# Up products with differences of weights, and a list scheduler that orders all engines

## The chip, the cores and the metric

The kernel runs on one core of one Trainium2 chip. The metric is the device time of one execution in microseconds (us). Three timed runs of the kernel before took 1724.11, 1726.66 and 1726.99 us; the median is 1726.66 us.

The engines are TensorE (PE; its weight loads are shown as PEld), VectorE (DVE), ScalarE (ACT), GpSimd (POOL) and SyncE (SP), whose queue issues transfers and, in this kernel, carries the marks between the two halves of a product. SBUF is the working memory and PSUM, with 8 banks of 128 x 512 float32, is where matmuls write.

## The reference

A causal convolution with weights of its own for each token and head is followed by a maxout layer.

```python
w = softmax(weight_gen, axis=-1)                      # 8 x 4160 tokens, 8 heads, 7 taps
out[b, s, h, :] = sum_k w[b, s, h, k] * x_pad[b, s + k, h, :]   # 192 = 8 heads x 24
x = out.reshape(33280, 192)
h = np.maximum(np.maximum(x @ w1, x @ w2), x @ w3)    # each weight 192 x 768
return h @ w_out                                      # 768 x 192
```

All is float32, and so is the result.

## The kernel before

**Tiles.** The 33280 tokens lie as 128 rows with 260 tokens each. Four tokens of each row, 512 in all, are a chunk, and there are 65 chunks; up to three chunks share the loading of x and of the tap weights and one softmax (a super). For each of the chunk's four token columns GpSimd multiplies taps and x (`product`, L244) and VectorE sums over the taps (`total`, L259). The sums are turned so that the 192 features lie on the partitions: the first three chunks on TensorE (L274, L275), the others by VectorE's transpose of 32 x 32 blocks (L282) and 24 small moves on ScalarE (L288).

**Parts.** TensorE multiplies in a short format (`F32R`), so each factor is split in a high part and a low part, and a product is high x high, low x high and high x low. `parts` makes them of x (L298 to L307): `xa_hi` and `xa_lo` for the first 128 features, and for the remaining 64, which fill only half of the partitions, `xb` and `xc` that hold the high part twice and the low part beside it. The weights are split once, at the start, by `split` (L459 to L487): ScalarE, six VectorE operations, ScalarE and GpSimd on each piece. They come as 8 byte words (`words`), so the splitting works on bits.

**Products.** Every product runs as two halves of 64 rows of the array: first the lower half's matmuls into a bank of PSUM, then the upper half's into the same bank. While the upper half of one product runs, the lower half of the next does. Between the two halves of one product stands an empty instruction on SyncE (L336), which waits for the lower half's last matmul and which the upper half's first waits for. `up` makes 18 products of 512 columns for a chunk, one for each of three weights and six blocks of 128 of the 768 columns, with 4 or 5 matmuls per half. `down` makes four, one for each token column, with twelve per half: `h_hi` against both parts of w_out side by side (384 columns) and `h_lo` against the high part (192).

**Maxout.** `maximum` empties the bank of the first weight by a ScalarE copy into `m` (L374), and takes the maxima with the second and the third on VectorE (L376). Then ScalarE casts `m` to `h_hi` (L379) and GpSimd subtracts to get `h_lo` (L383). A down sum's two column groups are added by ScalarE (L406) and VectorE (L407) and leave with one transfer for a chunk (L411).

**What sets the order.** Each engine runs its instructions in the order in which the program writes them (`pin`). That order is laid out by ticks: a chunk has 22, one for each half of a double product and one for each down sum, and constants name the chunk and the tick at which each stage is written (`PRODUCTS`, `SUMS`, `TRANSPOSE`, `PARTS`, `SOFTMAX`, `LOAD`). The first four chunks and the splitting of the weights have a table of their own, `OPENING`. The down sums of a chunk stand in the middle of the next one's up products (`DOWN_AT`). `lower` and `advance_upper` interleave the two halves by `SLOTS`. 

## Time and profile before

| | before |
|---|---|
| timed runs | 1724.11, 1726.66, 1726.99 us |
| span of the profiled execution, first to last instruction | 1723.8 us |
| PE busy | 1675.3 us, 97%, 16794 matmuls |
| PE weight loads busy | 1653.3 us, 96% |
| DVE busy | 1135.9 us, 66% |
| ACT busy | 1138.4 us, 66% |
| POOL busy | 1428.0 us, 83% |
| mean granted TensorE clock | 0.992 |
| moved by DMA | 79.50 MB, 46 GB/s in the mean |

The page gives the span of the profiled execution, and the three runs' device times beside it lie 0.3 to 3.2 us above. Matmuls overlap, so a busy PE says that matmuls were under way, not at what pace; the pace is read from the starts in the timeline. Groups of instructions are shown with count, total busy time and mean ns of one, and behind the bar with the idle time in front of them and what ended it. Stretches show the busy time of PE, PEld, DVE, ACT and POOL in a piece of the span, then the granted clock, the share of the DMA engines and GB/s.

### The profile page before, as it was taken

Reading aid. Unit: us, or ns where it says so; the run is one execution under the profiler, and the core shown is the slowest. Engines: PE = TensorE matmul, PEld = TensorE weight load, DVE = VectorE, ACT = ScalarE, POOL = GpSimd, SP = SyncE. Lnnn points to the kernel's source line nnn. Section 1 sums busy time; section 2 is a strip of 40 time slices with the busy share of each in tenths; the row PEclk is TensorE's granted clock in tenths of the full one; section 3 lists DMA queues with packets and bytes.
Section 4 is the critical chain, followed back from the end, with each engine's and each line's share of the span. In section 5 each row is a group of like instructions: output and inputs, shape, how many; then the busy total and the mean of one; then the engine's idle time right before and its main releaser. Section 6 shows DMA issues by size and latency. Waiting matters only on the chain.

```text
span 1723.8 us, 42110 instructions
## 1 busy us (share of the span) xinstructions
PE 1675.3 (97%) x16794; PEld 1653.3 (96%) x16794; DVE 1135.9 (66%) x1570; ACT 1138.4 (66%) x2878; POOL 1428.0 (83%) x844
## 2 busy tenths in 40 slices
PE   3789999999999999999999999999999999999998
PEld 2589999999999999999999999999999999999998
DVE  7976666666666666766666666666666666666652
ACT  4456676667667667666766766766676676676662
POOL 5788888988888888888888898988889888888852
PEclk9899999999999999999999999999999999999999
DMA  7010101101010101101010110101011010101000
GB/s 232 1 60 20 69 11 69 62 27 60 20 69 10 69 35 45 69 20 69 11 69 20 60 69 19 60 20 69 19 61 69 20 60 20 69 11 46 19 18 21
DMA packets 19989, 79.50 MB, mean 46 GB/s; under 512 B 2272, under 2 KB 4568, under 8 KB 17104
## 3 DMA queue, kind: packets, MB, share of 16 engines
q1 hardware_dynamic: 19672, 76.54, 11.6%
q8 instruction: 131, 2.15, 0.5%
q14 instruction: 66, 0.54, 0.1%
q10 hardware_dynamic: 120, 0.28, 0.1%
HBM read 51.25 MB, written 25.56 MB: 45 GB/s over the span
## 4 chain that ended last, share of the span: by engine, by line
PE 95%; DVE 3%; DMA 1%; ACT 1%; issue 0%; SPq 0%; POOL 0%; POOLq 0%; DVEq 0%; ACTq 0%
PE ph L327 95%; DVE acc L259 1%; DVE m L376 0%; DMA h_lo<-in_moe_w_dram 0%; DVE e L484 0%; DVE ph L480 0%; DVE ph L463 0%; DVE ph L475 0%; DVE ph L468 0%; DMA xt<-in_x_dram 0%; DVE ph L461 0%; SPq L518 0%; ACT ph L459 0%; ACT f L486 0%; PE ph L274 0%
## 5 line engine op out<-in xcount | busy, mean ns | idle before, releaser
L244 POOL TENSOR_TENSOR r<-xt,wt 128x1344 f32<-128x1344 f32 x260 | 721.9, 2816 | 1.9 <-DVE acc L259 1.4
L376 DVE TENSOR_TENSOR m<-ph,m 128x512 f32<-128x512 f32 x780 | 522.8, 684 | 219.7 <-PE ph L327 121.7
L383 POOL TENSOR_TENSOR h_lo<-m,h_hi 128x512 fp32r<-128x512 f32 x390 | 503.1, 1301 | 166.8 <-ACT h_hi L379 162.0
L327 PE MATMUL ph<-xa_hi,wa_hi 64*128 64x512 f32 x2340 | 628.6, 391 | 10.9 <-ACT f L486 7.0
L327 PE MATMUL ph<-xa_hi,wa_lo 64*128 64x512 f32 x2340 | 625.3, 389 | 5.8 <-POOL wa_lo L487 5.8
L327 PE MATMUL ph<-xa_lo,wa_hi 64*128 64x512 f32 x2340 | 625.0, 388 | 0.0
L327 PE MATMUL ph<-xb,wb_hi 64*128 64x512 f32 x2340 | 624.3, 388 | 0.0
L327 PE MATMUL ph<-wo,h_hi 64*128 64x384 f32 x3120 | 597.9, 360 | 0.2 <-DVE m L376 0.2
L327 PE MATMUL ph<-wo,h_lo 64*128 64x192 f32 x3120 | 556.6, 250 | 1.6 <-POOL h_lo L383 1.6
L379 ACT CAST h_hi<-m 128x512 fp32r<-128x512 f32 x390 | 241.9, 621 | 406.5 <-DVE m L376 403.4
L327 PEld LDWEIGHTS ph<-wo,h_hi 64*128 64x128 f32 x3120 | 488.6, 185 | 6.5 <-issue 1.0
L327 PEld LDWEIGHTS ph<-wo,h_lo 64*128 64x128 f32 x3120 | 487.1, 189 | 2.1 <-POOL h_lo L383 2.1
L259 DVE TENSOR_REDUCE acc<-r 128x192 f32<-128x1344 f32 x260 | 401.7, 1546 | 111.7 <-POOL r L244 111.7
L327 PE MATMUL ph<-xc,wb_lo 64*128 64x512 f32 x1170 | 453.6, 388 | 0.0
L288 ACT COPY room<-room 32x128 f32<-32x128 f32 x1488 | 440.6, 296 | 19.3 <-DVE room L282 1.2
L327 PEld LDWEIGHTS ph<-xa_hi,wa_hi 64*128 64x128 f32 x2340 | 366.3, 185 | 15.3 <-ACT f L486 8.2
L327 PEld LDWEIGHTS ph<-xa_hi,wa_lo 64*128 64x128 f32 x2340 | 358.6, 185 | 9.3 <-POOL wa_lo L487 7.9
L327 PEld LDWEIGHTS ph<-xa_lo,wa_hi 64*128 64x128 f32 x2340 | 359.0, 185 | 1.8 <-DVE xa_lo L302 0.4
L327 PEld LDWEIGHTS ph<-xb,wb_hi 64*128 64x128 f32 x2340 | 358.7, 185 | 1.4
L374 ACT COPY m<-ph 128x512 f32<-128x512 f32 x390 | 221.5, 585 | 60.5 <-PE ph L327 51.8
L407 DVE TENSOR_TENSOR o<-ph,ob 128x192 f32<-128x192 f32 x260 | 86.5, 352 | 238.5 <-ACT ob L406 238.5
L327 PEld LDWEIGHTS ph<-xc,wb_lo 64*128 64x128 f32 x1170 | 216.6, 185 | 1.2 <-issue 0.2
(57 smaller groups left out, 700.8 us busy)
## 6 DMA issues: line engine op xcount, KB each, us to landing
xt<-in_x_dram SPq DMA_DIRECT2D x20, 1728.0 KB, 6.9
out_dram<-o SPq DMA_DIRECT2D x65, 384.0 KB, 2.3
wt<-in_weight_gen_dram SPq DMA_DIRECT2D x21, 336.0 KB, 3.0
h_hi<-in_moe_w_dram SPq DMA_DIRECT2D x6, 256.0 KB, 5.2
xt<-in_x_dram SPq DMA_DIRECT2D x1, 1536.0 KB, 9.5
h_lo<-in_moe_w_dram SPq DMA_DIRECT2D x6, 192.0 KB, 5.2
room<-in_moe_w_out_dram SPq DMA_DIRECT2D x1, 1152.0 KB, 8.4
xt<-in_x_dram SPq DMA_DIRECT2D x1, 960.0 KB, 5.7
```

The lines of the kernel that those rows point to most:

```text
L244: nc.gpsimd.tensor_tensor(r.rearrange("p (h g) k -> p k h g", g=G), xt[:, la + t : la + t + K].rearrange("p k (h g) -> p k h g", g=G), wt[ ...
L259: nc.vector.tensor_reduce(state["acc", c][:, t], r, axis=AX.X, op=ALU.add)
L288: pin(nc.scalar.copy(to[:, :, p : p + 32], blocks[p : p + 32, :, f : f + 32]))
L327: ins = nc.tensor.matmul(ph[:, :n], w[h], v[h], start=half == 0 and q == 0, stop=half == 1 and q == len(terms) - 1,)
L374: pin(nc.scalar.copy(m[:, :N], ph[:, :N]))
L376: pin(nc.vector.tensor_tensor(m[:, :N], ph[:, :N], m[:, :N], op=ALU.max))
L379: later(1, lambda: pin(nc.scalar.copy(hi, m[:, :N])))
L383: nc.gpsimd.tensor_tensor(lo, m[:, :N], hi.bitcast(F32), op=ALU.subtract)
L407: pin(nc.vector.tensor_tensor(o[:, t], po[:, :D], ob, op=ALU.add))
```

## The change

**Arithmetic.** max(x w1, x w2, x w3) is x w1 + max(0, x (w2 - w1), x (w3 - w1)). So only two up products are made for each block, with the differences of the weights, and the first is emptied by a rectified copy on ScalarE (L859). The part x w1 reaches the output as x (w1 w_out): the 192 x 192 matrix w1 w_out is made once (`turn_weights`, `compose`) and three matmuls per half with the parts of x join each down sum (`wca`, `wcb`). The weights are needed as float32 for that: `single` rebuilds a float32 value from the words (ScalarE and four VectorE operations), GpSimd subtracts, ScalarE and GpSimd split.

**Emptying PSUM.** The second product's maximum (L867) is written back to its bank for four of the six blocks, and ScalarE's cast (L871) and the subtraction for `h_lo` (L878), which is then VectorE's, read it there. For blocks 1 and 4 (`ON_POOL`) it goes to `m`, and GpSimd subtracts as before.

**Loading.** Two chunks share x, tap weights and softmax instead of three. The second pieces of the weights are loaded in two groups (6 + 6 transfers instead of 6), w_out in three. Two chunks instead of three are turned on TensorE. The half of the partitions on which `xb` and the low part lie changes from chunk to chunk (`low`), which saves a copy of ScalarE (L306 of before).

**Order.** `OPENING` and the tick constants are gone. Each operation is a `Task` with an engine, a cost, the tasks that it needs, the buffers that it holds and a due time; `Plan.order` plays the engines through and starts, on each free engine, the ready task of earliest due time whose buffers are free. The two halves of TensorE are two engines there (L and U) and keep the order in which they are written. The instructions are then written in the order of these starts.

```diff
-OPENING = {
-    -1: (
...
-TICKS = 22
-PRODUCTS = ((2, 5), (2, 7), (2, 13), (2, 16))
-SUMS = ((2, 8), (2, 12), (2, 18), (1, 2))
-TRANSPOSE = ((1, 4), (1, 5), (1, 6), (1, 7), (1, 10), (1, 11), (1, 12))
-PARTS = ((1, 13), (1, 14), (1, 15))
-SOFTMAX = ((4, 13), (4, 20), (3, 13), (3, 15))
...
+        def can(t):
...
+                    h.taken = True
+                    self.free[h.pool] -= 1
+            t.start = now
+            done.append(t)
+            busy[t.engine] = now + t.cost
+            heapq.heappush(events, (now + t.cost, 0, t.n, t, "free"))
+            heapq.heappush(events, (now + t.end, 1, t.n, t, "given"))
+            heapq.heappush(events, (now + t.end + self.LATENCY, 2, t.n, t, "seen"))
+        now = 0.0
+        while True:
+            for e in ready:
+                if busy[e] > now + 1e-9:
+                    continue
+                if e in self.FIXED:
+                    k = at[e]
+                    if k < len(self.waiting[e]):
+                        t = self.waiting[e][k]
+                        if t.missing == 0 and can(t):
+                            at[e] += 1
+                            start(t, now)
+                    continue
+                heap, kept = ready[e], []
+                while heap:
+                    x = heapq.heappop(heap)
+                    if can(x[2]):
+                        start(x[2], now)
+                        break
+                    kept.append(x)
+                for x in kept:
+                    heapq.heappush(heap, x)
+            if not events:
+                break
+            now = events[0][0]
+            while events and events[0][0] <= now + 1e-9:
+                _, _, _, t, what = heapq.heappop(events)
+                if what == "given":
+                    for h in t.holds:
+                        h.users -= 1
+                        if h.users == 0:
+                            self.free[h.pool] += 1
+                elif what == "seen":
+                    for a in t.after:
+                        a.missing -= 1
+                        if a.missing == 0 and a.engine not in self.FIXED:
+                            heapq.heappush(ready[a.engine], (a.due, a.n, a))
+        assert len(done) == len(self.tasks), (len(done), len(self.tasks))
...
+    NI = 2
+    SC = 2
+    TS = SC * TC
+    ON_TENSOR = 2
+    DOWN_AT = 3
+    ON_POOL = (1, 4)
...
+            p = plan.add(
+                "POOL", 2.75, product, [ready[s], *loads[s][1]], due - 26 + 3 * t, [hr, hx, hw]
+            )
+            sums.append(plan.add("DVE", 1.55, total, [p], due - 22 + 3 * t, [hr, ha]))
...
+        lo = plan.add(name, cost, a_low, [hi], due - 1.5, [al, ah, *hs])
+        bl = plan.add(name, cost, b_low, cs, due - 1.4, [b, k, *hs])
...
+        a = plan.add(
+            "ACT", act(n),
+            lambda: pin(nc.scalar.activation(u(), high().bitcast(F32), AF.Abs)),
+            deps, due, [hb, hc, *holds],
+        )
...
+        return plan.add(
+            "DVE", vec(n),
+            lambda: pin(
+                nc.vector.scalar_tensor_tensor(
+                    target().bitcast(U32), low(), 29, ui(),
+                    op0=ALU.logical_shift_right, op1=ALU.bitwise_or,
+                )
+            ),
+            [d], due, [hb, hc, *holds],
+        )
...
+            d = plan.add(
+                "POOL", gps(2 * P),
+                lambda mine=mine: pin(
+                    nc.gpsimd.tensor_tensor(mine(), mine(), w1a[:, pair], op=ALU.subtract)
+                ),
+                [got, one_a[jp]], due - 3, [hx],
+            )
...
+            b = buf(hb)
+            pin(nc.tensor.transpose(b[:, :P], w1a[:, j], ident))
+            for to in (P, P + DB):
+                pin(nc.tensor.transpose(b[:, to : to + DB], b32[h, jp, 0], ident[h, h]))
+        got = plan.add("L", 0.5, turn, [one_a[jp], one_b[jp], made, *u_last()], 0, [hb], end=0.8)
...
+            def mult(hb=hb, at=at):
+                for j in range(NJ):
+                    pin(
+                        nc.tensor.matmul(
+                            buf(hb)[:, :D], w1t()[:, j, at : at + P], wo32[:, j],
+                            start=j == 0, stop=j == NJ - 1,
+                        )
+                    )
+            got = plan.add("L", 2.4, mult, deps + u_last(), 0, [hb, hw1t], end=2.8)
...
-            state["m", j] = mp.tile([P, CH], F32, name="m", bufs=4)
-        m = state["m", j]
-        if i == 0:
-            pin(nc.scalar.copy(m[:, :N], ph[:, :N]))
-        else:
-            pin(nc.vector.tensor_tensor(m[:, :N], ph[:, :N], m[:, :N], op=ALU.max))
-        if i == 2:
-            hi, lo = h_hi[:, j, :N], h_lo[:, j, :N]
-            later(1, lambda: pin(nc.scalar.copy(hi, m[:, :N])))
-            later(
-                2,
-                lambda: pin(
-                    nc.gpsimd.tensor_tensor(lo, m[:, :N], hi.bitcast(F32), op=ALU.subtract)
-                ),
-            )
+        def terms(half):
+            got = [
+                (CH, lambda: wa_hi[:, j, i], lambda: buf(ah), [w_hi[jp, i], hi], [ah]),
+                (CH, lambda: wa_hi[:, j, i], lambda: buf(al), [w_hi[jp, i], lo], [al]),
+                (
+                    (CH, lambda: wb_hi[:, j, i], lambda: buf(b), [*b_hi[j], bl], [b])
+                    if half == low
+                    else (CH, lambda: wb_hi[:, j, i], lambda: buf(k), [*b_hi[j], *cs], [k])
+                ),
+                (CH, lambda: wa_lo[:, j, i], lambda: buf(ah), [w_lo[jp, i], hi], [ah]),
+            ]
+            if half == odd:
+                got.append((CH, lambda: wb_lo[:, jp, i], lambda: buf(k), [b_lo[jp], *cs], [k]))
...
+        if i == 0:
+            hs[c, j, 0] = plan.add(
+                "ACT", act(CH),
+                lambda: pin(nc.scalar.activation(buf(hm), buf(hb), AF.Relu)), [made], due,
+                [hb, hm],
+            )
+            return
+        on_pool = j in ON_POOL
+        keep = hm if on_pool else hb
+        m = plan.add(
+            "DVE", vec(CH),
+            lambda: pin(nc.vector.tensor_tensor(buf(keep), buf(hb), buf(hm), op=ALU.max)),
+            [made, hs[c, j, 0]], due, [hb, hm],
+        )
+        his[j] = plan.add(
+            "ACT", act(CH), lambda: pin(nc.scalar.copy(buf(hh)[:, j], buf(keep))), [m], due + 1,
+            [keep, hh],
+        )
+        eng = nc.gpsimd if on_pool else nc.vector
+        los[j] = plan.add(
+            "POOL" if on_pool else "DVE", gps(CH) if on_pool else vec(CH),
+            lambda: pin(
+                eng.tensor_tensor(
+                    buf(hl)[:, j], buf(keep), buf(hh)[:, j].bitcast(F32), op=ALU.subtract
+                )
+            ),
+            [his[j]], due + 2, [keep, hh, hl],
+        )
...
-            terms += [(2 * D, h_hi[:, j, sl], wo[:, j]), (D, h_lo[:, j, sl], wo[:, j, :D])]
+        def terms(half):
+            got = [
+                (2 * D, lambda: buf(ah)[:, sl], lambda: wca, first, [ah]),
+                (D, lambda: buf(al)[:, sl], lambda: wca[:, :D], first, [al]),
+                (
+                    (D, lambda: buf(b)[:, sl], lambda: wcb[:, :D], first, [b])
+                    if half == low
+                    else (2 * D, lambda: buf(k)[:, sl], lambda: wcb, first, [k])
+                ),
+            ]
+            for j in range(NJ):
+                got.append(
+                    (
+                        2 * D, lambda j=j: buf(hh)[:, j, sl], lambda j=j: wo[:, j],
+                        [his[j], o_hi[j], o_lo[j]], [hh],
+                    )
+                )
+                got.append(
+                    (
+                        D, lambda j=j: buf(hl)[:, j, sl], lambda j=j: wo[:, j, :D],
+                        [los[j]], [hl],
+                    )
+                )
+            return got
...
+    for c in range(NC):
+        if c < ON_TENSOR:
+            tokens(c)
+        for j in range(NJ):
+            if c > 0 and j == DOWN_AT and c < NC - 1:
+                if c == 1:
+                    compose()
+                for t in range(TC):
+                    down(c - 1, t)
+            for i in range(NI):
+                up(c, j, i)
+        if c == 0:
+            for j in range(NJ):
+                turn_weights(j)
+        if c + 1 >= ON_TENSOR and c + 1 < NC:
+            tokens(c + 1)
```

TensorE, in the down sums of a chunk in mid-program. `wo` holds the parts of w_out, and `x2` stands for one matmul of each half. Before:

```order
L327 MATMUL ph<-wo,h_hi 128x384 x2
L327 MATMUL ph<-wo,h_lo 128x192 x2
L327 MATMUL ph<-wo,h_hi 128x384 x2
L327 MATMUL ph<-wo,h_lo 128x192 x2
L327 MATMUL ph<-wo,h_hi 128x384 x2
```

Now:

```order
L802 MATMUL bank<-wca,xa_hi 128x384
L802 MATMUL bank<-wo,h_hi 128x384
L802 MATMUL bank<-wca,xa_lo 128x192
L802 MATMUL bank<-wo,h_lo 128x192
L802 MATMUL bank<-wcb,xb 128x192
L802 MATMUL bank<-wo,h_hi 128x384 x2
L802 MATMUL bank<-wo,h_lo 128x192 x2
```

One half begins its three matmuls with x while the other ends its sums over h. In the other half the third of them is `wcb,xc` with 384 columns.

VectorE, one chunk in mid-program, from one transpose to the next. Before:

```order
L376 TENSOR_TENSOR m<-ph,m 128x512 x3
L259 TENSOR_REDUCE acc<-r 128x192
L376 TENSOR_TENSOR m<-ph,m 128x512 x2
L259 TENSOR_REDUCE acc<-r 128x192
L376 TENSOR_TENSOR m<-ph,m 128x512 x2
L213 TENSOR_REDUCE red<-wt 128x96
L376 TENSOR_TENSOR m<-ph,m 128x512
L407 TENSOR_TENSOR o<-ph,ob 128x192 x3
```

Now, the end of a chunk's blocks:

```order
L382 TENSOR_REDUCE acc<-r 128x192
L867 TENSOR_TENSOR bank<-bank,m 128x512 x2
L382 TENSOR_REDUCE acc<-r 128x192
L878 TENSOR_TENSOR h_lo<-bank,h_hi 128x512 x2
L867 TENSOR_TENSOR m<-bank,m 128x512
L867 TENSOR_TENSOR bank<-bank,m 128x512
L382 TENSOR_REDUCE acc<-r 128x192
L878 TENSOR_TENSOR h_lo<-bank,h_hi 128x512
L935 TENSOR_TENSOR o<-bank,ob 128x192
```

The maxima are half as many, and subtractions, each behind a cast of ScalarE, stand between them, with a sum over the taps in front of two of them.

ScalarE, at the start of the program, from the exponentials of the first chunk to the first parts of x. Before:

```order
L459 ACTIVATE ph<-h_hi 128x256
L473 CAST wa_hi<-ph 128x2x128
L459 ACTIVATE ph<-h_hi 128x256
L459 ACTIVATE ph<-h_lo 128x384
L473 CAST hi<-ph 128x384
L486 ACTIVATE f<-ph 128x384
L542 CAST wb_hi<-hi 64x384 x4
L298 CAST xa_hi<-ph 128x512
```

Now (the tiles `h_hi` and `h_lo` hold the weights' words here):

```order
L573 ACTIVATE bank<-h_hi 128x256 x3
L573 ACTIVATE bank<-h_lo 128x384
L573 ACTIVATE bank<-h_hi 128x256 x3
L335 ACTIVATE wt<-wt 128x448
L637 CAST wa_hi<-wx 128x2x128
L668 CAST bhi<-b_67 128x256
L684 CAST wb_hi<-bhi 64x256
L444 CAST xa_hi<-bank 128x512
```

The first steps of six pieces, of which the last three are the second third of wa, stand ahead of the first cast to `wa_hi`; before, one piece stood there.

More of the change, by code (lines that the diff above doesn't have):

```diff
@@ new lines, in lightconv_maxout_kernel @@
+    counts = {
+        "bank": 8, "xt": 2, "wt": 2, "red": 2, "den": 2, "r": 3, "acc": 2, "room": 1, "xa_hi": 2,
+        "xa_lo": 2, "xb": 2, "xc": 2, "m": 4, "h_hi": 2, "h_lo": 2, "ob": 2, "o": 2, "wx": 2,
+        "bhi": 2, "raw": 1,
+    }
+    pools = {
+        name: ctx.enter_context(
+            tc.tile_pool(
+                name=f"of_{name}",
+                bufs=n,
+                **({"space": bass.MemoryType.PSUM} if name == "bank" else {}),
+            )
+        )
+        for name, n in counts.items()
+    }
@@ L179, in pin, with vec, act, gps @@
         return ins
+    def vec(n):
+        return 0.15 + 0.00105 * n
+    def act(n):
+        return 0.18 + 0.00084 * n
+    def gps(n):
+        return 0.1 + 0.0024 * n
+    PERIOD = 21.0
+    FIRST = 22.0
+    def needed(c):
+        return FIRST + PERIOD * c
+    queue = {"SP": 0.0}
+    def transfer(cost, emit, deps=(), due=0.0, holds=(), on="SP"):
+        issue = plan.add(on, 0.45, emit, deps, due, holds)
+        return plan.add("DMA", cost, lambda: None, [issue], due, holds, end=cost + 2.0)
@@ L268, in transpose, with blocks @@
+    def blocks(c, ha, sums, wait):
+        due = needed(c)
         if c < ON_TENSOR:
-            pa, pb = (ps.tile([P, CH], F32, name="ph") for _ in range(2))
-            pb = pb[:DB]
-            state["p", c] = pa, pb
+            ba, bb = hold("bank"), hold("bank")
+            got = []
             for t in range(TC):
                 to = slice(t * P, (t + 1) * P)
-                pin(nc.tensor.transpose(pa[:, to], acc[:, t, :P], ident))
-                pin(nc.tensor.transpose(pb[:, to], acc[:, t, P:], ident))
-                yield
@@ new lines, in blocks, with move @@
+        turned = plan.add(
+            "DVE", 0.97, lambda: pin(nc.vector.transpose(places()[2], buf(ha))), sums, due - 12,
+            [hv, ha],
+        )
+        got = []
+        for q, f in enumerate(range(0, D, 32)):
+            for p in range(0, P, 32):
+                def move(f=f, p=p):
+                    pa, pb, b = places()
+                    to = pa[f : f + 32] if f < P else pb[f - P : f - P + 32]
+                    to = to.rearrange("f (t p) -> f t p", t=TC)
+                    pin(nc.scalar.copy(to[:, :, p : p + 32], b[p : p + 32, :, f : f + 32]))
+                got.append(plan.add("ACT", 0.296, move, [turned], due - 11 + q, [hv]))
@@ L382, in maximum @@
                 lambda: pin(
[L383 removed]
+                    nc.vector.tensor_tensor(buf(ho)[:, t], buf(hb)[:, :D], buf(hq), op=ALU.add)
                 ),
[L385 to L411 removed]
@@ new lines, in lightconv_maxout_kernel, with tokens @@
+    made = plan.add("POOL", 1.0, lambda: make_identity(nc, ident), (), -50)
+    for s in range(len(supers)):
+        load_super(s)
+    load_a(0)
+    load_b([0])
+    load_a(1)
+    load_b([1, 2])
+    load_a(2)
+    load_down()
+    for s in range(len(supers)):
+        softmax(s)
+    for jp in range(NP):
+        prepare_a(jp)
+        prepare_b(jp)
+    for q in range(NP):
+        prepare_down(q)
+    def tokens(c):
+        parts(c, *blocks(c, *taps(c), u_last() + [made]))
+    for c in range(ON_TENSOR, NC):
+        pass
@@ L655 @@
+    for c in (NC - 2, NC - 1):
+        for t in range(TC):
+            down(c, t)
+    for t in plan.order():
+        t.emit()
 _INS = ["x", "weight_gen", "moe_w1", "moe_w2", "moe_w3", "moe_w_out"]
```

981 lines of the change are left out of this document (547 added, 434 removed).

## The prediction

> **What bounds the kernel now.** I read the chain of waits first, then the busy time by stretches, then single rows of TensorE's timeline.
>
> ```profile
> PE 95%; DVE 3%; DMA 1%; ACT 1%; issue 0%; SPq 0%; POOL 0%; POOLq 0%; DVEq 0%; ACTq 0%
> 28.31 4.93 PE ph L327 x17
> 70.06 4.88 PE ph L327 x26
> 96.17 1609.13 PE ph L327 x13585
> 1709.30 10.55 PE ph L327 x83
> 80.00:100.00 20.00, 14.99 (x139) 12.69 (x137) 14.72 (x23) 6.60 (x14) 16.33 (x13) 0.91 0.00 1
> 1000.00:1100.00 100.00, 100.00 (x1022) 99.67 (x1020) 67.20 (x92) 68.79 (x177) 88.04 (x51) 1.00 0.10 39
> ```
>
> The first row is the chain by engine, the next four are pieces of it (start, length, what), the last two are stretches with the busy time of PE, PE's weight loads, DVE, ACT and POOL. From 96.17 us to 1705 us the chain is matmuls and nothing else, at granted clock 1.00, while the best helper is POOL with 88%. So the time is matmul work, an opening of 96 us and a short end. TensorE's timeline gives the price of each kind of work (start, length of one matmul):
>
> ```profile
> 1006.34 0.33 PE L327 MATMUL ph<-wo,h_hi 64*128 64x384 f32 x1
> 1013.28 0.42 PE L327 MATMUL ph<-xa_hi,wa_hi 64*128 64x512 f32 x1
> 1031.69 0.33 PE L327 MATMUL ph<-wo,h_hi 64*128 64x384 f32 x1
> ```
>
> These are the lower half's starts of a chunk's down sums, of the up products behind them, and of the next chunk's down sums. One chunk takes 1031.69 - 1006.34 = 25.35 us. Four down sums take 6.94 us: per half 24 pairs of a 384 and a 192 wide matmul, 0.289 us a pair. Eighteen up products take 18.41 us, 1.023 us each. The two halves overlap, so a half's pace is the pace.
>
> **The cut on TensorE.** A chunk now has 12 up products: 12 x 1.023 = 12.27 us. A down sum grows per half from 12 to 15 matmuls, of both halves together 15 of each width, so 7.5 pairs: 4 x 7.5 x 0.289 = 8.68 us. The split of 0.289 between the widths is not shown, and isn't needed, since the added matmuls are as many wide as narrow. Together 20.95 us, 4.40 us less; over 65 chunks 286 us, which taken from the span of 1723.8 leaves 1438 if nothing else moved. I check this below from the other side, stage by stage.
>
> **Whether the helpers keep that pace.** Work per chunk after, from these rows (count, total and mean ns):
>
> ```profile
> L376 DVE TENSOR_TENSOR m<-ph,m 128x512 f32<-128x512 f32 x780 | 522.8, 684 | 219.7 <-PE ph L327 121.7 <-ACT m L374 81.6
> L302 DVE TENSOR_TENSOR xa_lo<-ph,xa_hi 128x512 fp32r<-128x512 f32 x3 | 2.1, 688 | 2.2 <-ACT xa_hi L298 2.2
> L259 DVE TENSOR_REDUCE acc<-r 128x192 f32<-128x1344 f32 x260 | 401.7, 1546 | 111.7 <-POOL r L244 111.7
> L407 DVE TENSOR_TENSOR o<-ph,ob 128x192 f32<-128x192 f32 x260 | 86.5, 352 | 238.5 <-ACT ob L406 238.5
> L282 DVE STREAM_TRANSPOSE room<-acc 128x768 f32<-128x768 f32 x62 | 60.1, 969 | 0.1
> L213 DVE TENSOR_REDUCE red<-wt 128x96 f32<-128x672 f32 x21 | 17.7, 842 | 0.0
> L288 ACT COPY room<-room 32x128 f32<-32x128 f32 x1488 | 440.6, 296 | 19.3 <-DVE room L282 1.2
> L374 ACT COPY m<-ph 128x512 f32<-128x512 f32 x390 | 221.5, 585 | 60.5 <-PE ph L327 51.8 <-POOL xb L307 6.9
> L379 ACT CAST h_hi<-m 128x512 fp32r<-128x512 f32 x390 | 241.9, 621 | 406.5 <-DVE m L376 403.4
> L406 ACT COPY ob<-ph 128x192 f32<-128x192 f32 x260 | 73.8, 314 | 50.3 <-PE ph L327 33.7 <-DVE o L407 16.6
> L244 POOL TENSOR_TENSOR r<-xt,wt 128x1344 f32<-128x1344 f32 x260 | 721.9, 2816 | 1.9 <-DVE acc L259 1.4 <-DMA xt<-in_x_dram 0.3
> L383 POOL TENSOR_TENSOR h_lo<-m,h_hi 128x512 fp32r<-128x512 f32 x390 | 503.1, 1301 | 166.8 <-ACT h_hi L379 162.0
> L302 POOL TENSOR_TENSOR xa_lo<-room,xa_hi 128x512 fp32r<-128x512 f32 x62 | 80.3, 1295 | 24.8 <-ACT xa_hi L298 24.8
> L215 POOL TENSOR_TENSOR wt<-wt,red 128x672 f32<-128x672 f32 x21 | 28.8, 1371 | 49.7 <-DVE red L213 47.2 <-PE ph L327 2.5
> ```
>
> VectorE: 6 maxima at 0.684, 4 subtractions from PSUM (the row L302 is the same form) at 0.688, 4 sums at 1.546, 4 adds at 0.352, one transpose at 0.969, and softmax, about 1.0 (two reductions of two thirds of 0.842 and the small operations, halved for two chunks): 16.4 us. ScalarE: 24 moves at 0.296, 6 rectified copies and 4 casts out of PSUM at the copy's 0.585, 2 casts at 0.621, three casts of x at 0.62 instead of four, 4 copies at 0.314, 0.3 of exponentials: 17.6 us. GpSimd: 4 products at 2.816, 2 subtractions at 1.301, xa_lo and xb at 1.295, softmax 0.97: 17.4 us. All three lie under 20.95, between 78% and 84%, so none is a bound by its sum. The rectified copy and the maximum that is written back to PSUM do not occur before; between the PSUM copy's 0.585 and the cast's 0.621 the first moves ScalarE's sum by 0.2 us, so it can't change the order.
>
> Order could still cost. The bank of a second product is now held until h_lo is made: two halves of 1.02, 0.684, 0.585 and 0.688, so 4.0 us bare, some 2 us by which the lower half may run ahead, and the waits in the queues. The eighth product behind it wants the bank, 8 x 1.023 = 8.2 us later, which leaves about 2 us for waits. One sum of 1.546 in front of the maximum or of the subtraction fits; two and a cast (3.7 us) don't. And the x of the next chunk can be split only when the last down sum has read its x, since there are two buffers: that is 6.1 + 8.7 of the lower half and 0.6 for the upper one's first matmuls, 15.4 us into a chunk of 20.95. From then ScalarE's 0.62 and GpSimd's two times 1.295 need 3.3 us with their hand-overs. It fits by 2.2 us, and is 0.6 us late where a product of 2.816 has just begun. I take 0 to 0.3 us a chunk, and of that 3 us in all. [...]
>
> **The opening.** Weights are now made in two steps. Six VectorE operations for each piece become four, and the sums of x remain:
>
> ```profile
> L461 DVE TENSOR_SCALAR ph<-ph 128x256 f32<-128x256 f32 x9 | 3.8, 423 | 2.3 <-ACT ph L459 2.3
> L463 DVE TENSOR_SCALAR ph<-ph 128x384 uint32<-128x384 uint32 x3 | 1.7, 566 | 0.1
> 7.29 3.90 SPq L518 DMA_DIRECT2D h_lo<-in_moe_w_dram  x6
> 14.62 8.92 SPq L200 DMA_DIRECT2D xt<-in_x_dram  x8
> L274 PE MATMUL ph<-ident,acc 128*128 128x128 f32 x12 | 4.8, 410 | 26.0 <-DVE acc L259 26.0
> ```
>
> VectorE's order up to chunk 1's xa_lo holds 36 operations of 256 (15.4 us), 24 of 384 (13.5), ten sums and two more behind (18.6), six maxima and four subtractions (6.9), and softmax, zeroing, a transpose and chunk 0's x parts (about 8.8): 63 us. Idle comes on top. SyncE must issue six more weight pieces, and the second third of wa now stands behind the eight small x transfers, which took 8.92 us to issue: the pieces before them end at about 11, so it is issued near 21 and lands near 26. ScalarE's order has the three first steps of that third ahead of the cast of the first wa_hi. So VectorE waits about 7 us, and TensorE starts near 29.8 instead of 28.31. With 3 us of other waits chunk 1 begins at 63 + 7 + 3 = 73, against 70.06 in the row above. The cheaper splitting is thus used up by the late transfers and by work that was later before.
>
> Behind three blocks of chunk 1 (6.1 us) comes the product of w1 and w_out: 12 full-array matmuls and two hand-overs. No row has this; 128 columns of 32 bit took 0.41, so 0.6 for 192 columns and 7.4 for all is the upper end, and a 512 wide matmul's 0.11 each, 1.3, the lower. I take 5, nearer the first, whose type it shares, less some overlap. With 1.4 for the upper half to end and 2 for the split of the result, no matmul runs for 8.4 us (4.7 to 10.8). The first down sum starts at 73 + 6.1 + 8.4 = 87.5, against 96.17.
>
> **Sum.** 62 periods of 20.95 lead to the down sums inside chunk 63: 87.5 + 1298.9 = 1386.4. There remain those (8.7), 6 up products (6.1), chunk 64 (12.3), two chunks of down sums (17.4): 1430.9; the last upper half 2.5; from the last matmul to the end 3.95, as 1709.30 + 10.55 leaves to 1723.8. With the 3 us of waits the span is 1440. The stall of the old end, POOL's last h_lo, is gone, since chunk 63's down sums now lie in front of it. The timed runs stand 0.3 to 3.2 us above the profiled span of 1723.8, their median 2.9; I add 2.5 and say **1443 us**.
>
> **Rivals.**
> First, the helpers don't keep pace: a bank or an x part comes late in each chunk. For: three engines near 80%, in fixed order, with sums of 1.5 us that nothing can break. Against: the slack of 2 us above. 0.3 to 1.5 us a chunk is 20 to 97 us: 1463 to 1540.
> Second, the opening. If the chain through the late transfers stretches by a third, chunk 1 begins at 95 and the time is 1465; if waits overlap and it begins at 60, 1430.
> Third, the change does not cut what it says, since TensorE is paced by the number of matmuls: 25.35 / 258 = 0.098 us each, now 228, so 22.4 us a chunk and 1537. Against: 162 up matmuls in 18.41 us are 0.114 each, 96 down matmuls 0.072, so width counts.
> Fourth, slower than before. The upper half of every product waits for an empty instruction on SyncE's queue, and the transfers of out, weights and x stand in the same queue, each put there as soon as the kernel's scheduler thinks its buffer free. A transfer that waits for VectorE or GpSimd holds the next products' marks, and TensorE. It decides from 4.4 us a chunk; at 5 us the time is 1443 + 65 x 5 = 1768. Against: a transfer's issue is 0.3 to 0.5 us here, and once TensorE is held, the late engine catches up, so a wait does not repeat in full.
>
> **How the numbers follow.** The forecast has 0.76, with its own range from 1428 to 1460; the first rival 0.11, the second 0.08, the third 0.02, the fourth 0.03. The range runs from 1426 (a good opening) into the first rival up to 1482. A measurement tells 0.2%, 3.5 us, from no change: faster 0.96, same 0.01, slower 0.03.
>
> **What would show it.** Down sums of neighbouring chunks 20.95 us apart; stretches in mid-program with PE at 100% and about 1088 matmuls in 100 us; chunk 1's first matmul near 73 and the first down sum near 88. A period over 21.3 with idle time ahead of matmuls that VectorE or ScalarE ends speaks for the first rival, one ended by SyncE for the fourth. The forecast falls if the period isn't between 20.8 and 21.3, or if the opening is off by over 15 us.

## The result, and the profile after

| | before | changed |
|---|---|---|
| timed runs, median | 1726.73 us (1724.11 to 1726.99) | 1444.69 us (1438.88 to 1445.39) |
| ratio to before | | 0.8366, interval 0.8349 to 0.8382 |
| span of the profiled execution | 1723.8 us | 1442.8 us (its own time 1444.6) |
| chunk 1's up products, start in the chain | 70.06 us | 72.73 us (predicted 73) |
| from chunk to chunk | 25.36 us | 20.90 us (predicted 20.95) |

The forecast was 1443 us. One execution in all that follows, of the kernel with both edits below, was slow (1691.79 us at a mean clock of 0.753) and is left out of its median.

The chain of waits of the changed kernel, by engine, with the pieces that answer to those shown of before (start, length, what):

```profile
PE 95%; POOL 1%; DMA 1%; ACT 1%; SPq 1%; DVE 1%; issue 0%; POOLq 0%
...
28.23 5.18 POOL r L370 x2
33.41 0.60 POOL wa_lo L643
34.06 5.53 PE bank L802 x18
...
72.73 4.65 PE bank L802 x11
...
87.88 4.04 DVE den L344
92.22 1347.23 PE bank L802 x12536
```

From 92.22 us to the end but for 3.4 us the chain is matmuls without a break, as before from 96.17 to 1705. Two matmuls of chunk 1 run ahead of 72.73, at 70.88 and 71.61. What isn't matmul lies in the opening, and one row in it was in no step of the prediction: 4.04 us of `den` on VectorE, a sum with a constant over 64 columns.

Stretches of the changed kernel (busy PE, PEld, DVE, ACT, POOL, then granted clock, DMA share, GB/s):

```profile
71.00:77.00 6.00, 5.68 (x17) 4.12 (x19) 3.04 (x6) 4.72 (x14) 1.37 (x2) 0.50 0.00 0
73.00:92.00 19.00, 14.00 (x78) 12.12 (x78) 12.62 (x14) 11.05 (x31) 15.37 (x8) 0.86 0.01 1
92.00:100.00 8.00, 7.78 (x43) 7.78 (x45) 3.48 (x4) 0.00 (x0) 5.22 (x2) 0.50 0.00 0
800.00:900.00 100.00, 100.00 (x1099) 99.22 (x1096) 76.16 (x102) 83.74 (x213) 81.27 (x43) 1.00 0.19 69
```

In mid-program TensorE is never idle, and the helpers are busy for 76%, 84% and 81% (predicted 78%, 84% and 83% of a period). Behind the pause at 88 to 92 us the clock is granted at 0.50: 43 matmuls in 8 us, where 800 to 900 us has 88 in the same time. It is at 0.50 from 71 to 77 us too, where chunk 1 begins.

The lower half's first matmul of neighbouring chunks' down sums, in TensorE's timeline:

```profile
977.15 0.33 PE L802 MATMUL bank<-wca,xa_hi 64*128 64x384 f32 x1
...
997.92 0.33 PE L802 MATMUL bank<-wca,xa_hi 64*128 64x384 f32 x1
...
1018.94 0.33 PE L802 MATMUL bank<-wca,xa_hi 64*128 64x384 f32 x1
```

The distances are 20.77 and 21.02, 20.90 in the mean; they alternate, as does the half that has the wide matmul with `xc`.

Groups of the changed kernel (count, total and mean ns, then idle time in front):

```profile
L867 DVE TENSOR_TENSOR bank<-bank,m 128x512 f32<-128x512 f32 x260 | 179.0, 689 | 42.2 <-PE bank L802 24.3 <-ACT m L859 9.3 <-ACT h_hi L871 1.4
L859 ACT ACTIVATE m<-bank 128x512 f32<-128x512 f32 x390 | 234.5, 601 | 71.4 <-PE bank L802 66.7
L344 DVE TENSOR_SCALAR den<-den 128x64 f32<-128x64 f32 x32 | 35.5, 1108 | 1.0
L750 PE MATMUL bank<-wo,raw 128*128 128x192 f32 x24 | 4.2, 330 | 0.0
```

The maximum that is written back to PSUM costs what the other form cost (0.689 against 0.684), the rectified copy 0.601, as bounded. The product of w1 and w_out appears as 24 records of 0.330, in 4.2 us; 5 us were taken for it. The sum with a constant takes 1.108 us in the mean; before, on 96 columns, its median was 0.403 (below).

### The profile page after: what moved, and what is told of

It is laid out like the page before. It is cut to its first block, busy times and chain, and to the rows that moved or that the text cites. A ratio compares the mean times of both kernels' runs of the same rounds, so it can differ in the third digit from the quotient of the medians.

```text
span 1442.8 us, 37119 instructions
## 1 busy us (share of the span) xinstructions
PE 1402.0 (97%) x14878; PEld 1366.1 (95%) x14878; DVE 1043.4 (72%) x1433; ACT 1117.3 (77%) x2828; POOL 1104.2 (77%) x609
## 4 chain that ended last, share of the span: by engine, by line
PE 95%; POOL 1%; DMA 1%; ACT 1%; SPq 1%; DVE 1%; issue 0%; POOLq 0%
PE bank L802 95%; POOL r L370 1%; DMA xt<-in_x_dram 1%; SPq L532 1%; DVE den L344 0%; ACT room L432 0%; DMA raw<-in_moe_w_dram 0%; SPq L516 0%; PE bank L733 0%; ACT m L859 0%; POOL wa_lo L643 0%; PE bank L731 0%; ACT wb_hi L684 0%; DVE acc L382 0%; ACT bank L573 0%
## 5 line engine op out<-in xcount | busy, mean ns | idle before, releaser
L802 PE MATMUL bank<-wo,h_hi 64*128 64x384 f32 x3120 | 675.0, 357 | 0.0
L802 PE MATMUL bank<-wo,h_lo 64*128 64x192 f32 x3120 | 603.4, 249 | 0.0
L802 PEld LDWEIGHTS bank<-wo,h_lo 64*128 64x128 f32 x3120 | 493.0, 188 | 0.0
L802 PEld LDWEIGHTS bank<-wo,h_hi 64*128 64x128 f32 x3120 | 489.2, 186 | 0.0
L802 PE MATMUL bank<-xa_hi,wa_hi 64*128 64x512 f32 x1560 | 479.9, 394 | 6.0 <-ACT wa_hi L637 3.4
L802 PE MATMUL bank<-xa_hi,wa_lo 64*128 64x512 f32 x1560 | 477.9, 390 | 3.4 <-POOL wa_lo L643 3.3
L802 PE MATMUL bank<-xa_lo,wa_hi 64*128 64x512 f32 x1560 | 476.8, 391 | 0.5 <-DVE xa_lo L460 0.5
L859 ACT ACTIVATE m<-bank 128x512 f32<-128x512 f32 x390 | 234.5, 601 | 71.4 <-PE bank L802 66.7
L802 PE MATMUL bank<-xb,wb_hi 64*128 64x512 f32 x780 | 284.5, 390 | 0.3 <-DVE xb L465 0.3
L802 PE MATMUL bank<-xc,wb_hi 64*128 64x512 f32 x780 | 281.1, 390 | 0.2 <-ACT wb_hi L684 0.2
L867 DVE TENSOR_TENSOR bank<-bank,m 128x512 f32<-128x512 f32 x260 | 179.0, 689 | 42.2 <-PE bank L802 24.3
L878 POOL TENSOR_TENSOR h_lo<-m,h_hi 128x512 fp32r<-128x512 f32 x130 | 171.7, 1321 | 40.0 <-ACT h_hi L871 39.9
L878 DVE TENSOR_TENSOR h_lo<-bank,h_hi 128x512 fp32r<-128x512 f32 x260 | 172.4, 681 | 11.4 <-ACT h_hi L871 11.2
```

The source lines that it names most:

```text
L802: ins = nc.tensor.matmul(buf(hb)[:, :n], w()[h], v()[h], start=half == 0 and first, stop=half == 1 and last,)
L859: lambda: pin(nc.scalar.activation(buf(hm), buf(hb), AF.Relu)), [made], due,
L867: lambda: pin(nc.vector.tensor_tensor(buf(keep), buf(hb), buf(hm), op=ALU.max)),
L878: eng.tensor_tensor(buf(hl)[:, j], buf(keep), buf(hh)[:, j].bitcast(F32), op=ALU.subtract)
```

## What the pause at the first down sum is made of

VectorE and GpSimd around that pause, in the timeline of the changed kernel:

```profile
84.07 7.80 POOL L370 TENSOR_TENSOR r<-xt,wt 128x1344 f32<-128x1344 f32 x3
...
86.57 0.32 ACT L759 CAST wcb<-bank 128x192 fp32r<-128x192 f32 x1 [0.98 <-PE bank L750]
...
87.79 4.12 DVE L344 TENSOR_SCALAR den<-den 128x64 f32<-128x64 f32 x1
91.82 0.34 DVE L767 TENSOR_TENSOR wcb<-bank,wcb 128x192 fp32r<-128x192 f32 x1
...
92.22 0.28 PEld L802 LDWEIGHTS bank<-wcb,xc 64*128 64x128 f32 x1 [5.45 <-DVE wcb L767]
```

ScalarE's half of `wcb` is ready at 86.89. VectorE's half stands behind a sum over the taps and `den` in its order, and `den` ends at 91.91, as GpSimd's run of three products does (84.07 + 7.80 = 91.87). TensorE needs `wcb` in the first down sum and waits until 92.22. In TensorE's timeline the last matmul that the lower half has of chunk 1's three blocks, and the product of w1 and w_out, are

```profile
80.73 0.39 PE L802 MATMUL bank<-xc,wb_lo 64*128 64x512 f32 x1
82.37 4.17 PE L750 MATMUL bank<-wo,raw 128*128 128x192 f32 x24
```

So the 19.5 us from 72.73 to 92.22 have four parts. Three blocks at full clock are 6.1. They took 8.2 (to 80.73 and a step of 0.23), 2.1 more: the clock is at 0.50 until 77.5. The matrix itself, from there to 87.23 (86.89 and 0.34 for VectorE's half), takes 6.3: the upper half's end, the 24 matmuls, the split. The last 5.0 are the place of `wcb` in VectorE's order, 4.0 of them `den`.

Does that small sum wait for GpSimd, or is it just slow? All its executions, in both kernels and in the first experiment below, in which it has another form (shortest, median and longest in ns):

```profile
L223 DVE TENSOR_SCALAR den<-den x23: 181/403/799, 6.2 to 1618.5; 128x96 f32<-128x96 f32 x21, 128x32 f32<-128x32 f32 x2
```

```profile
L344 DVE TENSOR_SCALAR den<-den x33: 181/1186/4124, 7.4 to 1278.4; 128x64 f32<-128x64 f32 x32, 128x32 f32<-128x32 f32 x1
```

```profile
L346 DVE TENSOR_REDUCE den<-den x33: 186/220/220, 7.3 to 1269.4; 128x64 f32<-128x64 f32 x32, 128x32 f32<-128x32 f32 x1
```

With the timeline beside them: of the 33 in the changed kernel, 29 began while a GpSimd instruction ran, and 28 of these ended 0.04 to 0.06 us behind the end of such an instruction, after 0.25 to 4.12 us. The one exception began 0.04 us ahead of the end and took 0.20. The four with GpSimd idle took 0.18 to 0.20. Before, 20 of 23 began under a product of GpSimd and ended with it, but the order had put them near its end: 19 took 0.38 to 0.45, one 0.80, and the three with GpSimd idle 0.18 to 0.21. So theory A: this form waits for GpSimd, here on the path. Theory B: the pause is set by something else, such as the loads or the matrix itself, and the sum only fills it.

## The experiments

**The changed kernel again**, as the measure for the next three on one chip.

> The changed kernel unaltered, as the yardstick for the three runs beside it. Expected 1444.7 us; its four runs so far gave 1438.88 and 1444.60 to 1445.39, so a spread of some 6 us belongs to it.

Measured: 1443.87 us (1440.33 to 1445.95), ratio 0.8365 (0.8354 to 0.8376). Here `den` took 1.29 us and chunk 1 began at 74.72, and the unbroken chain began at nearly the same time, 92.16. What varies between runs lies in the opening, the clock above all: here it was at 0.50 from 51 to 81.7 us without a break.

**The small sum in a form that does not wait.** A reduction over one element stands in place of the sum; the 1e-9 in the softmax's denominator is left out, here and wherever this edit is part of a kernel.

```diff
-            "DVE", 0.3, lambda: pin(nc.vector.tensor_scalar_add(part(hd), part(hd), 1e-9)),
+            "DVE", 0.3,
+            lambda: pin(
+                nc.vector.tensor_reduce(part(hd), part(hd).unsqueeze(2), axis=AX.X, op=ALU.add)
+            ),
```

> In softmax VectorE's addition of 1e-9 to the sums (L344, SBUF to SBUF, median 1.19 us and once 4.12 us, where the same form took 0.18 to 0.8 before) is replaced in the same place by a reduction over one element, which leaves the value as it is, since each sum is at least 1 and float32 does not hold 1 + 1e-9. Order and everything else stay. Theory A: this form of VectorE instruction waits for GpSimd's running instruction; the 4.12 us ended with GpSimd's run of three products, and held wcb, for which the first down sum waited 5.2 us. Then the replaced operation takes under 0.3 us each, the wait at wcb falls to about 1 us, and the time to 1436 to 1441. Rival B: the small matrix's split and its hand-over cost the 5 us themselves; then the wait stays, and the time is within 2 us of the changed kernel's.

Measured: 1437.85 us (1435.65 to 1442.22), ratio 0.8336 (0.8324 to 0.8347), 6.0 below the run above. The timeline of this run, at the same place:

```profile
81.89 7.83 POOL L373 TENSOR_TENSOR r<-xt,wt 128x1344 f32<-128x1344 f32 x3
...
85.42 0.21 DVE L346 TENSOR_REDUCE den<-den 128x64 f32<-128x64 f32 x1
85.55 0.35 DVE L770 TENSOR_TENSOR wcb<-bank,wcb 128x192 fp32r<-128x192 f32 x1
```

Under the same three products the small operation takes 0.21 and `wcb` follows at once. Theory A holds for the wait. The size is not all its own: of 7.6 us between the two profiled spans, chunk 1 begins 4.2 earlier (70.48), of which 1.4 are there at `wa_lo` and the rest varies between runs of one kernel (72.73 and 74.72 above); from there to the unbroken chain (85.95) it is 2.0 shorter, 1.3 of that by the clock in chunk 1's blocks and 0.7 by the wait for `wcb`; and the clock behind is at 0.57 for 4 us instead of 0.50 and 0.65 for 8, which saves 1.7. The mean clock of a run goes with its time. Of the changed kernel's eight runs the two at 0.991 and 0.992 took 1440.33 and 1438.88, the six at 0.985 to 0.987 1443.30 to 1445.95. Here three of four have 0.990 or 0.991, and the one at 0.987 took 1442.22. So at an equal clock the edit is worth some 2 to 5 us, by few runs; whether it also makes the higher clock more frequent isn't shown.

**The next chunks' x and tap weights loaded later.** GpSimd's first products (28.23 in the chain above) stand ahead of `wa_lo`, for which TensorE waits until 34.06.

```diff
-        due = needed(cs[0]) - 40
+        due = needed(cs[0]) - (34 if s == 1 else 40)
```

> The second pair of chunks' taps and x, with the eight small transfers, are due 6 us later in the scheduler, so they are issued behind all three thirds of wa and wb; this also lets the scheduler move the first steps of the second third on ScalarE. Theory A: the late second third of wa and the softmax and products in front of the first wa_lo delay the opening; then its last first step on ScalarE comes near 16 instead of 23.86 us, TensorE's stall at 31.7 to 34.1 us shrinks, and chunk 1 begins at 66 to 69 instead of 72.7, 4 to 7 us earlier in the end. Rival B: VectorE's 63 us of work up to chunk 1 bind the opening; then chunk 1 begins at 71 to 74 again and the time stays within 2 us.

Measured: 1439.74 us (1438.89 to 1440.41), ratio 0.8343 (0.8332 to 0.8354), 4.1 below. Chunk 1 begins at 68.53, as theory A had it, and TensorE's wait up to 34.06 is gone (matmuls again from 30.11). One of its signs failed: of ScalarE's first steps on the second third of wa, two come at 14.56 and 15.23, but the last not until 26.50, later than 23.86. That points to GpSimd's order as what made room, more than to the arrival of the weights. `den` (2.34 us there) still stands ahead of `wcb`, with which the pause ends at 86.48.

**Both edits.**

> Both edits. If each theory A holds, the gains add: some 8 to 13 us less than the changed kernel, 1432 to 1437. If only one holds, its gain alone.

Measured: 1436.08 us (1434.64 to 1442.50), ratio 0.8327 (0.8313 to 0.8342). That is 7.8 below, not the sum of 10.1: chunk 1 begins at 70.30 and the unbroken chain at 86.33, no earlier than with one of the edits. What lies between chunk 1's beginning and the unbroken chain, over the 6.1 us of three blocks, is in the profiled runs, split as above (us):

| | blocks longer, by the clock | the matrix | `wcb` in VectorE's order | in all |
|---|---|---|---|---|
| changed | 2.1 | 6.3 | 5.0 | 13.4 |
| the same again | 3.2 | 6.2 | 1.9 | 11.3 |
| small sum as a reduction | 1.9 | 6.2 | 1.2 | 9.4 |
| loads later | 1.5 | 6.3 | 4.1 | 11.9 |
| both | 1.7 | 6.3 | 2.0 | 9.9 |

The matrix takes the same everywhere, and the next run moves it.

**That product ahead of chunk 1**, with both edits above. `tokens` makes chunk 1's x parts, and TensorE waits for them.

```diff
         if c < ON_TENSOR:
             tokens(c)
+        if c == 1:
+            compose()
         for j in range(NJ):
             if c > 0 and j == DOWN_AT and c < NC - 1:
-                if c == 1:
-                    compose()
```

> Change: both edits before, and the product of w1 and w_out is written ahead of chunk 1's up products instead of behind three blocks of them. Theory A (the pause at the first down sum is the making of that matrix, and only where it stands makes it cost): its 24 matmuls and two hand-overs then lie where TensorE waits for chunk 1's x anyway, and no break of over 1 us stands at the first down sum. The time falls by the bubble's remainder, 6 to 8 us, to 1429 to 1431. Theory B (weights for the matrix or VectorE's order are what is late, not the place): chunk 1's first matmul is pushed back by as much as the bubble gives, and the time stays at 1437.

Measured: 1426.34 us (1425.06 to 1428.56), ratio 0.8268 (0.8255 to 0.8280); 9.7 below the run with both edits, more than the 6 to 8 expected. Its chain of waits:

```profile
66.68 5.40 PE bank L753 x24
72.08 1347.83 PE bank L805 x12779
```

and its stretch over the first down sums:

```profile
72.00:92.00 20.00, 20.00 (x207) 19.50 (x208) 13.85 (x20) 13.34 (x35) 19.25 (x11) 1.00 0.01 2
```

The matrix takes 5.40 us where TensorE waited in part for chunk 1's x, so that chunk 1's third matmul, with which it began above, starts only 2.3 us later than with both edits (72.58, against 70.30). No pause follows, and the first down sum's matmul with `wcb` starts at 78.77 instead of 86.33, 7.6 us earlier. The clock has a part in that: chunk 1's blocks run at 1.00 here, and with both edits at 0.50 up to 74.3. Behind the wait for `wcb`, 2.20 us with both edits, that run has

```profile
87.85:94.60 6.75, 6.75 (x47) 6.75 (x47) 1.55 (x1) 0.32 (x1) 6.75 (x4) 0.50 0.00 0
```

which costs half of it, 3.4 us; here the clock is 1.00.

**That edit alone**, on the changed kernel.

> Change against the changed kernel: only the place of the product of w1 and w_out, ahead of chunk 1's up products. Theory A (what the pause at the first down sum costs is its length, 13.3 us from the end of chunk 1's first three blocks to 92.2 less the 5 of the matmuls, which move into an idle stretch, and 4.5 more by the clock that is granted at 0.50 behind it): no pause over 1 us and no stretch under 0.9 behind chunk 1's first matmul; with VectorE's late sum and the early x loads still there, chunk 1 begins at 72 to 76, and the time is 1444.7 - 12 = 1432 +- 3, some 6 above the run with all three edits. Theory B (the two other edits made the room for it): chunk 1 begins at 78 or later, 1437 or more.

Measured: 1429.14 us (1426.53 to 1435.10), ratio 0.8282 (0.8264 to 0.8300). Against the changed kernel's 0.8366 that is 0.0084 of 1726, 14.5 us less. Theory A holds, at the end of its range: chunk 1 begins at 75.19 and the chain of matmuls isn't broken from there. The interval overlaps that of the run with all three edits, so the other two, worth 6.0 and 4.1 us alone, add nothing here that this measurement tells for certain; in the profiled runs chunk 1 begins 3.1 us later without them.

**The price of what was added: no products with x in the down sums.**

```diff
-            got = [
-                (2 * D, lambda: buf(ah)[:, sl], lambda: wca, first, [ah]),
...
-            ]
+            got = []
```

> Left out: the three matmuls per half with x in each down sum, so the output lacks x (w1 w_out). It measures the price of what was added. By width (the step of the prediction: 1.5 pairs per half at 0.289, four sums, 1.73 us a chunk) the period falls from 20.90 to 19.17 and the time by 113 us, to about 1332. By the number of matmuls (24 fewer of 228 at 0.0917) it falls by 2.2 to 18.7, by 143 us, to about 1302. If the helpers (ScalarE 17.6, GpSimd 17.4 us a chunk) then bind, the period stays between 19.3 and 20.5 with idle time of TensorE, 1340 to 1420.

Measured, one run: 1321.21 us. Starts of the down sums:

```profile
1007.29 0.33 PE L802 MATMUL bank<-wo,h_hi 64*128 64x384 f32 x1
...
1026.36 0.33 PE L802 MATMUL bank<-wo,h_hi 64*128 64x384 f32 x1
```

19.07 us, so the added matmuls cost 20.90 - 19.07 = 1.83 us a chunk; by width 1.73 was expected, by number 2.2. But for three chunks early on (20.1 to 21.2 us) the helpers do not bind at this pace either:

```profile
800.00:900.00 100.00, 100.00 (x1089) 100.00 (x1088) 79.71 (x110) 89.11 (x231) 87.48 (x47) 1.00 0.19 69
```

The time is 11 us below what the width gives: 6.5 are 65 times the difference of the prices. The other 4.5 are in the trace: the first inner sums over h start at 87.18 instead of 92.70, without the wait for `wcb`, and the first period, at 19.32, is only 0.25 over the later ones instead of 4.06; of these 9.3 us the three early chunks take back 4.7.

**The price of what was removed: a third up product for each block.**

```diff
-            for i in range(NI):
-                up(c, j, i)
+            for i, more in ((0, False), (1, True), (1, False)):
+                up(c, j, i, more)
```

> Added: a third up product for each block (the third weight once more, which changes no maximum) and its maximum on VectorE; the scheduler's period is set to 27.2. It measures the price of what was removed. By width (6 x 1.023 = 6.14 us a chunk) the period rises to 27.04 and the time by 399 us, to about 1844. By the number of matmuls (54 more at 0.0917) it rises by 4.95 to 25.85 and the time by 322, to about 1767.

Measured, one run: 1826.97 us. Starts of the down sums:

```profile
1009.04 0.33 PE L802 MATMUL bank<-wca,xa_hi 64*128 64x384 f32 x1
...
1036.24 0.33 PE L802 MATMUL bank<-wca,xa_hi 64*128 64x384 f32 x1
...
1063.10 0.33 PE L802 MATMUL bank<-wca,xa_hi 64*128 64x384 f32 x1
```

27.03 us in the mean of the two (27.00 over 61 chunks): six products cost 6.13, where 6.14 was expected by width and 4.95 by number. The time is 17 below the expectation. Its first down sums over h begin at 88.47 with three more products in front of them, where the changed kernel's 92.70 with these 3.1 us would be 95.8: 7.3 us of the 17 lie there. Chunk 0's six added products, in an opening in which TensorE waits anyway, may be another 6; that is argued and not measured.

**TensorE's work of before under the new order**: both edits together.

> The third up product of the run before, and the three matmuls with x left out (the output lacks x (w1 w_out)); the scheduler's period is 25.4. TensorE then has the matmuls of the kernel before, under the new order. Theory A (all of the gain is the matmuls removed, the new order gives nothing): the period is 25.3 to 25.4 and the time 1727 +- 12. Theory B (the new scheduler gives part of the gain, or takes some): a period off by 0.3 us or more, the time off by over 20 us.

Measured: 1724.09 us (1723.13 to 1724.59), ratio 0.9991 (0.9982 to 1.0001). By time theory A: all that is new but the number of matmuls, which is the scheduler, the emptying of PSUM and the loading together, gives nothing in sum. But amounts cancel in it. Chunk 1's down sums start at 110.00 us, against 118.83 before, and before's stall ahead of its last matmuls (1705.3 to 1709.3) is gone. Its period is 25.19 us up to 788 us and 25.8 in the mean behind, 25.55 over all, against 25.36, which is 11.6 us on 61 chunks: the chain there passes through VectorE's maxima and ScalarE, with three products to empty for each block. Why it changes in mid-program stays open.

**All of h_lo on GpSimd.**

```diff
-    ON_POOL = (1, 4)
+    ON_POOL = tuple(range(6))
```

> Change: the maxima of all six blocks go to m and GpSimd makes all six h_lo. GpSimd's work is then 17.4 + 4 x 1.30 = 22.6 us a chunk, over TensorE's 20.9. Theory A (the helpers do not bind at 84%, but bind by their sum as soon as it passes TensorE's): the period is 22.6 to 23.2, GpSimd is busy over 97% and TensorE waits in every chunk: 1444 + 65 x 1.7 to 2.3 = 1555 to 1595. Theory B (a release of banks sooner, since the subtraction leaves PSUM, gives time back): a period of 20.9 to 21.3.

Measured, one run: 1552.28 us, 3 us below the range of theory A; the period, 22.85 in the mean, lies in it. The loss does not come in each chunk, as theory A had it: nine of ten lie between 20.8 and 23.6 us, and the tenth is 34 to 35 us long, presumably when GpSimd has fallen behind by as much as the buffers hold. One such place, and the ten chunks around it:

```profile
963.00:993.00 30.00, 23.02 (x215) 19.96 (x212) 17.04 (x21) 17.67 (x44) 28.58 (x17) 0.90 0.18 68
880.00:1110.00 230.00, 222.41 (x2285) 212.68 (x2285) 133.37 (x172) 172.42 (x437) 218.34 (x132) 0.98 0.15 54
```

GpSimd is busy for 218.34 of 230 us, 95%, not the 97% expected. So a helper binds once its sum (22.6 us, an estimate from the prediction's rows) passes TensorE's 20.9, and 84% is not near.

**Seven banks of PSUM**, and then six.

```diff
-        "bank": 8, "xt": 2, "wt": 2, "red": 2, "den": 2, "r": 3, "acc": 2, "room": 1, "xa_hi": 2,
+        "bank": 7, "xt": 2, "wt": 2, "red": 2, "den": 2, "r": 3, "acc": 2, "room": 1, "xa_hi": 2,
```

> Change: 7 banks of PSUM instead of 8. By the prediction's step a bank is wanted again 8 x 1.02 = 8.2 us after it was taken, with about 2 us to spare; with 7 it is 7.15 us, 1 us to spare. Theory A (that slack is real): the period grows by 0 to 0.15 us, the time by 0 to 10 us. Theory B (the eight banks are already just enough, so the forecast held by luck): 0.5 us or more a chunk, over 30 us.

Measured, one run: 1446.47 us, period 20.91. The eighth bank's 1.02 us was slack.

> Change: 6 banks instead of 8. A bank is then wanted again after 6.1 us, as long as or less than the estimate of 6 for its hold (two halves, the maximum, the cast, the subtraction and 2 us of lead). Theory A: TensorE waits for banks in each chunk, 0.5 to 2 us, period 21.4 to 22.9, time 1477 to 1575, idle time ahead of matmuls ended by VectorE or ScalarE. Theory B (the hold is shorter than estimated, 5 us or less): no more than 0.2 us a chunk, under 1460.

Measured, one run: 1522.07 us, period 22.25, so theory A, 1.35 us a chunk. Its chain, in every second chunk:

```profile
990.40 1.30 POOL xb L465
...
991.77 1.30 POOL xa_lo L460
...
993.09 0.99 DVE room L421
...
995.66 0.61 ACT m L859
...
996.31 38.42 PE bank L802 x344
...
1040.81 9.24 PE bank L802 x72
```

Not the second product's long hold of a bank ends the wait, as the prediction's chain had it, but the first one's copy: it stands in ScalarE's order behind moves of `room`, these behind VectorE's transpose, and that behind GpSimd's parts of x, which wait for the last down sum that reads the old x. The stretch in mid-program hides it:

```profile
800.00:900.00 100.00, 99.60 (x1041) 95.31 (x1039) 71.43 (x95) 78.48 (x201) 77.61 (x42) 1.00 0.18 66
```

PE is busy 99.6%, since one half of the array has matmuls under way while the other waits. Only the number of matmuls, 1041 instead of 1099, tells of it.

## Why the prediction was right, step by step

| step | predicted | measured |
|---|---|---|
| 12 up products | 12.27 us | 12.26 (six cost 6.13) |
| four down sums | 8.68 | 8.64 (the rest of 20.90) |
| of that, the products with x | 1.73 | 1.83 |
| helpers late, in all | 3 | 0 (no wait behind 92.22) |
| TensorE's start | 29.8 | 26.33, but 34.06 with `wa_lo` |
| chunk 1 | 73 | 72.73 (74.72 in the second profile) |
| its first three blocks | 6.1 | 8.2, by the half clock |
| pause behind them | 8.4 | 11.3: 6.3 and the wait of 5.0 for `wcb` |
| half clock behind the pause | none | 4.1 |
| down sums inside chunk 63 | 1386.4 | 1391.98 |
| from there to the end of the span | 51.0 (44.5 + 2.5 + 3.95) | 50.8 |

**The cut on TensorE** was priced right: width sets the pace of both kinds of product. That rejects the third rival, by number of matmuls, from both sides (1.83 against 2.2, 6.13 against 4.95), and it is the whole gain: with the matmuls of before all the rest of the change gives 0.9991.

**The helpers** keep pace, so the first rival falls, and the reason given holds: their sums lie well under the period. TensorE keeps it at 89% of ScalarE, and loses it with GpSimd at 95%. The 2 us of slack for a bank are bracketed by the runs with seven banks (nothing lost) and six (1.35 us a chunk). So the emptying of PSUM sets the pace with six banks (a period of 22.25 us) and not with eight (20.90). The chain that the prediction gave for a bank's hold was the wrong one, as the run with six banks showed.

**SyncE's marks** (the fourth rival) end 1.4 us of TensorE's weight loads' idle time in the whole run.

**The opening** hit 73 in good part by luck. The late second third of wa was not what held TensorE but `wa_lo` behind GpSimd's softmax and two products (27.20 to 33.41). VectorE, whose work was to fill 63 of the 73 us, was busy for 56.2 of the first 72.7, and did not bind: with the loads due later chunk 1 begins at 68.53. And the 96.17 that the prediction sets beside its first down sum isn't before's first: two of chunk 0's four had run from 85.63. That number is in no term of the sum.

**The step that failed** is "no matmul runs for 8.4 us (4.7 to 10.8)", and with it the full clock that the sum takes for granted. What the step counted takes less, 6.3 us (4.2 for the matmuls, where 5 were taken). Two things are missing in it. `wcb` stands behind a sum over the taps and `den` in VectorE's order, and `den` waits for GpSimd: 5.0 us. And the clock is at 0.50 around the pause: 2.1 us in chunk 1's blocks ahead of it, and 4.1 behind it, where the first period is 24.96 us instead of 20.90. The 2.1 too little and the 2.1 too much cancel, which leaves 9.1 us. Against these stand the period's 0.05 on 61 chunks (3.1), the 3 us for late helpers that didn't come, 0.3 of the opening, 0.7 by which the timed run lies nearer to its span than was taken (1.8 for 2.5), and small amounts, so that the forecast was off by 1.7 us. That they cancel is luck, though none was big enough to leave the range. The two large ones were in one place, and moving one piece of code there gains 14.5 us, over eight times the forecast's total error.

## What to carry to other kernels

A gain on the engine that bounds can be priced from the starts of neighbouring matmuls alone, as long as each helper's sum stays under the new period; test that by taking away a buffer or loading one helper more, since a busy share near 100% hides a lost pace (99.6% with six banks, which lost 1.35 us a chunk). Serial work that needs TensorE once belongs where TensorE waits anyway, and a pause cost its length here and a slow clock behind it (5.2 us without a matmul, then 0.50 until 101.4 us, which cost 4.1). When a small VectorE operation takes several times its shortest time (here 1.11 us in the mean and up to 4.12, against 0.18), look at what GpSimd does at its end.

## What the runs showed of the hardware

A sum with a constant on VectorE, from SBUF to SBUF in float32, did not run beside a GpSimd instruction here: of 29 that began under one, 28 ended with GpSimd's work, after up to 4.12 us, and a reduction in its place took 0.21 us under the same products. In the longest of them VectorE began to wait at 87.79, in the second of three products in a row, which ended at 89.36, and got through only at 91.91, with the third.

```profile
86.59 2.77 POOL L370 TENSOR_TENSOR r<-xt,wt 128x1344 f32<-128x1344 f32 x1
```

```profile
89.11 2.75 POOL L370 TENSOR_TENSOR r<-xt,wt 128x1344 f32<-128x1344 f32 x1
```

So it can be kept waiting past the instruction that it met. It need not be: at 25.66 it met one that ended at 25.86, with another behind it, and was done at 25.91.

Behind the pause of the changed kernel TensorE's clock stays low. The first two stretches are of that kernel, the third of the run with the reduction:

```profile
91.20:101.30 10.10, 9.08 (x53) 9.08 (x53) 4.29 (x5) 0.00 (x0) 5.89 (x3) 0.50 0.00 0
101.40:104.00 2.60, 2.60 (x37) 2.60 (x38) 1.82 (x2) 0.79 (x2) 0.00 (x0) 1.00 0.00 0
88.45:91.75 3.30, 3.30 (x28) 3.30 (x27) 0.77 (x1) 0.00 (x0) 3.30 (x2) 0.50 0.00 0
```

Idle time of 5.2 us comes with 10.2 us at 0.50 (91.1 to 101.4), with matmuls under way all the time from 92.22 (14 of them up to 96 us); 2.2 us (both edits) are followed by 6.8 us (87.8 to 94.6), and 1.3 us (the reduction) by 3.4 (88.4 to 91.8). These are three, two and one times 3.4 us. In the last two the clock falls 1.5 and 2.4 us after matmuls have begun again. What makes the clock fall, and what sets how long it stays low, these runs don't show.
